# Spectral mixing and a snake MLP on one Trainium2 core: PSUM dealt out by hand, and a burst's halves evicted in one instruction each

## The chip, the cores and the metric

The kernel runs on one core of one Trainium2 chip. The core has TensorE (matrix multiplication, written PE in the profile, its weight loads PEld), VectorE (DVE), ScalarE (ACT), GpSimd (POOL, here mainly an issuer of DMAs) and SyncE (SP, another issuer of DMAs). They run side by side and wait for one another through semaphores. Matmul results land in PSUM, eight banks that hold 512 fp32 columns for each of 128 partitions; VectorE or ScalarE then copies them out ("evicts" them). The metric is device time in microseconds.

## The reference

The input `x` has 8 batches of 3008 positions and 256 channels. It passes a spectral filter along the positions and then a two-layer MLP with a snake activation:

```python
X = np.fft.rfft(x, axis=1)
F = (filt_r + 1j * filt_i)[None, :, :]
y = np.fft.irfft(X * F, n=x.shape[1], axis=1)
h = y.reshape(24064, 256) @ w_in            # 256 -> 2048
s = np.sin(alpha * h)
g = h + s * s / (alpha + 1e-09)
out = g @ w_out                             # 2048 -> 256
```

## The kernel before

**The Fourier part.** 3008 = 47 x 64, so each transform is done in two matmul stages with a pass through DRAM between them. For each batch the stages are: `first` (length 47, tile `pa`), a store to DRAM (`d1`) and a load back in another order (`t2`), `forward` (length 64, tile `pb`, cast to `xf`), the filter product on VectorE (`product`, `cross`; the part that needs swapped halves goes through two SyncE transfers into `xs`), `inverse` (tile `pc`, cast to `g` or `gt`), a store to DRAM (`d2`) and a load (`t4`), and `last` (tile `pd`, cast into `y`). Batch 0 has its own code at the start, batch 1 uses the whole array, and the batches 2 to 7 use the array in quarters.

**Bursts.** For the batches 2 to 7 the stages `first` and `inverse` are written so that four matmuls of a 64x64 quarter of the array can run at once. One call of `first_tiled` issues 8 matmuls, one call of `inverse_tiled` 16. There are 6 x 4 = 24 of the first (called forward bursts below) and 6 x 3 = 18 of the second (inverse bursts), 42 in all. A burst writes four PSUM tiles of 512 columns: two passes q = 0, 1 and in each one tile for each half of the array's rows (h in `first_tiled`, k in `inverse_tiled`). Pass 0 takes both its tiles from the pool `fps`, pass 1 both from `hps`. Each pass is followed in program order by its two evictions. A forward burst has two on ScalarE (h = 0) and two on VectorE (h = 1), an inverse burst three on ScalarE and one on VectorE.

**The MLP part.** The positions are worked through in chunks of 512 (some of 384). For a chunk, `hidden(k, jb)` makes one block of 128 hidden features: two matmuls into a tile `ph` of `hps` (line 601), a cosine on ScalarE into one of four slots of `cos_all` (605), and a VectorE instruction that forms the snake's result `v` from the cosine and from `ph` (606); here sin² is had from a cosine, with the factors folded into the weights. `project(k - 1, u)` multiplies the previous chunk's `v` by the second weight matrix into a tile `po` of `ops` (620), ScalarE copies that to `o` (630), and DMAs store it (665).

**PSUM.** Three pools share the eight banks: `fps` with two tiles, `hps` with four, `ops` with two. Apart from the bursts, `fps` serves `forward` and `last` in the main part, one bank for each call, and `hps` serves `hidden`. A pool hands its banks out in turn; an instruction that writes a bank waits until the bank's last reader is done.

**Order.** Nothing reorders instructions: the program order is written out by hand. The main loop takes steps; a step has two calls of `hidden` (four ph matmuls), a slot, one or more half blocks of `project` (eight po matmuls each), and a second slot. The Fourier stages stand in a list sorted by due time (`put`) and are issued in the slots, normally one TensorE stage for each slot. `clear` moves `forward` and `last` away from the slot of a burst, to a step later, and `aside` moves VectorE's products. Each engine works through its own queue in this order; on SyncE the stores to DRAM, the transfers for `xs` and the loads of `t4` share one queue.

**Who evicts.** `evac` copies a tile out on the engine that its caller names. Where none is named, a counter decides: it goes up by one with every call, whoever makes it, and each third call goes to VectorE. Of the main part's stages only `last` (the casts into `y`) leaves it to the counter.

Of the kernel before, what the change touches and what calls it, by code (L numbers as in the profile page):

```python
# [9 lines left out]
FP16 = mybir.dt.float16  # L10
# [10 lines left out]
N1, N2 = 47, 64  # L21
# [50 lines left out]
def kernel(  # L72
# [44 lines left out]
    dpool = pool("dram", 2, DRAM)  # L117
    fps = pool("fps", 2, PSUM)
    hps = pool("hps", 4, PSUM)
    ops = pool("ops", 2, PSUM)  # L120

# [67 lines left out]
    class Spectral:  # L189
# [13 lines left out]
        def first(self, i):  # L203
            ch, j = divmod(i, 4)
            ps = fps.tile([128, 512], FP32, name=f"pa_{self.b}_{i}", tag="f")
            marks["pe"] = nc.tensor.matmul(out=ps[0:NK, :], lhsT=wf_t, rhs=self.x[ch][:, 2 * j:2 * j + 2, :],
                                           start=True, stop=True)
            r0 = 8 * (ch % 2)
            evac(t1_h[ch // 2][0:NK, r0 + 2 * j:r0 + 2 * j + 2, :], ps[0:NK, :])
            if j == 3:  # L210
                nc.sync.dma_start(out=self.d1_rows[:, 8 * ch:8 * ch + 8, :], 
                                  in_=t1_h[ch // 2][0:NK, r0:r0 + 8, :])

        def first_tiled(self, ch):
            r0 = 8 * (ch % 2)
            for q in range(2):
                own, tag = (hps, "h") if q else (fps, "f")
                ps = [own.tile([128, 512], FP32, name=f"pa_{self.b}_{ch}_{q}_{h}", tag=tag) for h in range(2)]
                for h in range(2):
                    for c in range(2):  # L220
                        n = 4 * c + 2 * q
                        nc.tensor.matmul(out=ps[h][64 * c:64 * c + 64, :], lhsT=wt_t[64 * h:64 * h + N1],  # L222
                                         rhs=self.x[ch][64 * h:64 * h + N1, n:n + 2, :], start=True, stop=True)
                for h in range(2):
                    evac(t1_h[ch // 2][:, r0 + 4 * h + 2 * q:r0 + 4 * h + 2 * q + 2, :], ps[h], h == 0)
            d1 = self.d1.rearrange("a (h n) c -> a h (n c)", h=2)
            for c in range(2):
                n0 = (8 * ch + 4 * c) * C
                nc.sync.dma_start(out=d1[:, :, n0:n0 + 4 * C],
                                  in_=t1_h[ch // 2][64 * c:64 * c + 2 * NS, r0:r0 + 8, :]  # L230
                                  .rearrange("a (h n) c -> a h (n c)", h=2))
# [6 lines left out]
        def forward(self, u):  # L238
            b = self.b
            ps = fps.tile([128, 2, C], FP32, name=f"pb_{b}_{u}", tag="f")  # L240
            for i in range(2):
                s = 2 * u + i
                nc.tensor.matmul(out=ps[:, i, :], lhsT=d_t[:, s, :],  # L243
                                 rhs=self.t2[s // 6][:, s % 6, :], start=True, stop=True)
# [21 lines left out]
        def inverse(self, w):  # L266
            b = self.b
            pr = self.p.pop(w)
            if w % 3 == 0:
                self.g = gpool.tile([128, 6, C], FP16, name=f"g_{b}_{w}", tag="g")  # L270
            ps = fps.tile([128, 2, C], FP32, name=f"pc_{b}_{w}", tag="f")
# [12 lines left out]
        def inverse_tiled(self, w):  # L284
            g = gpool.tile([128, 4, 2, C], FP16, name=f"gt_{self.b}_{w}", tag="g")
            for q in range(2):
                own, tag = (hps, "h") if q else (fps, "f")
                ps = [own.tile([128, 2, C], FP32, name=f"pc_{self.b}_{w}_{q}_{k}", tag=tag) for k in range(2)]
                for i in range(2):
                    for k in range(2):  # L290
                        for c in range(2):
                            u = 4 * w + 2 * c + q
                            nc.tensor.matmul(out=ps[k][64 * c:64 * c + 64, i, :],  # L293
                                             lhsT=eh_t[64 * k:64 * k + 64, 2 * u + i, :],
                                             rhs=self.p[u][0][64 * k:64 * k + 64, i, :], start=True, stop=True)
# [52 lines left out]
    def spread_alpha(i):  # L348

        ps = hps.tile([128, 4, 128], FP32, name=f"al_bc_{i}", tag="h")  # L350
        for a in range(4):
# [40 lines left out]

    def last_0(n0, n, own=fps, tag="f", spread=False):

        for cb in range(2):
            made = []

            def one(i, cb=cb, made=made):

                if i == 0:  # L400
                    ps = own.tile([128, 512], FP32, name=f"pd_0_{n0}_{cb}", tag=tag)
                    made.append(ps[:, 0:n * NR].rearrange("p (a r) -> p a r", r=NR))
                nc.tensor.matmul(out=made[0][:, i, :], lhsT=t4_cols[:, n0 + i, :, cb], rhs=wi0_t,
# [10 lines left out]
    def reciprocals():  # L414

        ps = ops.tile([128, 512], FP32, name="ps_rec", tag="o")
        nc.tensor.transpose(out=ps[:, 0:16], in_=rec, identity=id32)
        nc.vector.tensor_scalar(out=rec_t, in0=ps[:, 0:16], scalar1=-0.5, scalar2=None, op0=ALU.mult)

    def inverse_table(g):  # L420

        gs = slice(8 * g, 8 * g + 8)
        ps = ops.tile([128, 8, 128], FP16, name=f"pse_{g}", tag="o")
        for i in range(8):
# [4 lines left out]

    warmed = []  # L430

    def warm_pe(n):

        warmed.append(n)
        ps = hps.tile([128, 512], FP32, name=f"warm_{len(warmed)}", tag="h")
        for i in range(n):
# [19 lines left out]
    for i in range(16):  # L456
        own, tag = (fps, "f") if i % 3 == 2 else (hps, "h")
        ps = own.tile([128, 512], FP32, name=f"pa_0_{i}", tag=tag)
        nc.tensor.matmul(out=ps, lhsT=wf0_t[0:NR], rhs=x0[i // 4][:, 2 * (i % 4):2 * (i % 4) + 2, :],  # L459
# [27 lines left out]
    def forward_0(i):  # L487
        hc, w = blocks[i]
        ps = hps.tile([128, 4, 128], FP32, name=f"pb_0_{i}", tag="h")
        for j in range(4):  # L490
# [16 lines left out]
    def inverse_0(i):  # L507
        hc, w = blocks[i]
        ps = fps.tile([128, 4, 128], FP32, name=f"pc_0_{i}", tag="f")
        for j in range(4):  # L510
# [73 lines left out]
    last_0(0, 4)  # L584
    last_0(4, 2, hps, "h")
    warm_pe(2)
# [23 lines left out]
    def project(k, u):  # L610
# [6 lines left out]
        if (t % 2 == 0 or final) and half == 0:  # L617
            pso[k] = ops.tile([128, 2, C], FP32, name=f"po_{k}_{t}", tag="o")
        for jb in range(8 * half, 8 * half + 8):
# [79 lines left out]
    for n0, n, at in ((6, 5, 1.5), (11, 4, 11), (15, 4, 13), (19, 4, 15.5), (23, 4, 17), (27, 5, 19)):  # L699
        put(at, last_0, n0, n, fps, "f", True)  # L700
    for b in range(1, B):
# [90 lines left out]
```

## Time and profile before

| What | Value |
|---|---|
| Median of the runs | 778.87 us |
| Lowest of the runs | 777.43 us |
| Profiled execution, its own time | 779.97 us |
| its span, first to last instruction | 778.2 us |
| Granted TensorE clock, mean | 0.997 |
| Matmuls ph (line 601) | 1536, 0.216 us apart in a row |
| Matmuls po (line 620) | 3008, 0.109 us apart in a row |
| Forward burst, 8 matmuls | 0.63 us from its first start to its last end |
| Inverse burst, 16 matmuls | 0.63 us |
| VectorE cast of 128x512 from PSUM | 0.682 us |
| ScalarE cast of 128x512 from PSUM | 0.59 us |
| ScalarE cosine 128x512 / VectorE snake 128x512 | 0.608 / 0.682 us |

Times of a single instruction run from its shown start to its shown end; instructions that follow one another on an engine overlap a little, so a group of two or three is shorter than its sum. A matmul is shown with its way through the array (0.379 us for 512 columns), although the next can start 0.216 us after it. In the chain of work that ended last each piece is counted from the end of the piece before it. The span leaves out 1.8 us of the execution's own time.

### The profile page before, as it was taken

Reading aid. Unit: us, or ns where it says so; the run is one execution under the profiler, and the core shown is the slowest. Engines: PE = TensorE matmul, PEld = TensorE weight load, DVE = VectorE, ACT = ScalarE, POOL = GpSimd, SP = SyncE. Lnnn points to the kernel's source line nnn. Section 1 sums busy time; section 2 is a strip of 40 time slices with the busy share of each in tenths; the row PEclk is TensorE's granted clock in tenths of the full one; section 3 lists DMA queues with packets and bytes.
Section 4 is the critical chain, followed back from the end, with each engine's and each line's share of the span. In section 5 each row is a group of like instructions: output and inputs, shape, how many; then the busy total and the mean of one; then the engine's idle time right before and its main releaser. Section 6 shows DMA issues by size and latency. Waiting matters only on the chain.

```text
span 778.2 us, 17224 instructions
## 1 busy us (share of the span) xinstructions
PE 763.9 (98%) x6039; PEld 517.3 (66%) x6039; DVE 658.2 (85%) x1173; ACT 610.5 (78%) x1203; POOL 371.2 (48%) x649
## 2 busy tenths in 40 slices
PE   8999999999999999999999999999999999999997
PEld 4757766666666666666666666766666666766665
DVE  6986998999988888898889988899888888787773
ACT  5798888898888877888878787788778787777762
POOL 6355554634555655455464647554464655430000
PEclk9999999999999999999999999999999999999999
DMA  9955578854765428644474536764254332411112
GB/s 227 264 110 158 119 179 240 223 137 124 188 164 133 124 58 215 157 108 128 108 202 111 141 93 147 198 150 121 72 145 111 85 72 56 135 46 34 36 41 56
DMA packets 81518, 101.49 MB, mean 130 GB/s; under 512 B 18884, under 2 KB 60864, under 8 KB 81431
## 3 DMA queue, kind: packets, MB, share of 16 engines
q0 software_dynamic: 27440, 47.29, 25.9%
q1 hardware_dynamic: 53434, 52.79, 25.3%
q8 instruction: 47, 0.77, 0.4%
q10 hardware_dynamic: 557, 0.31, 0.2%
q14 instruction: 40, 0.33, 0.1%
HBM read 56.15 MB, written 46.66 MB: 132 GB/s over the span
## 4 chain that ended last, share of the span: by engine, by line
PE 91%; DVE 4%; DMA 2%; ACT 1%; issue 1%; ACTq 0%; POOLq 0%; DVEq 0%
PE po L620 40%; PE ph L601 40%; DVE v L606 3%; PE pd L316 2%; PE pb L243 2%; PE pa L222 2%; PE pc L293 1%; PE pc L513 1%; DMA w<-in_moe_alpha_dram 1%; PE warm L437 1%; DMA d<-t_h 1%; ACT cos_all L605 1%; PE pb L491 1%; DMA t<-d 1%; PE pa L459 1%
## 5 line engine op out<-in xcount | busy, mean ns | idle before, releaser
L606 DVE SCALAR_TENSOR_TENSOR v<-cos_all,ph 128x512 f16<-128x512 f32 (+1 forms) x768 | 482.7, 671 | 96.9 <-ACT cos_all L605 93.1
L605 ACT ACTIVATE cos_all<-ph 128x512 f32<-128x512 f32 (+1 forms) x768 | 413.7, 599 | 100.3 <-PE ph L601 99.8
L665 POOL DMA_DIRECT2D out_dram<-o x530 | 292.5, 558 | 241.8 <-ACT o L630 212.6
L601 PE MATMUL ph<-y,w 128*128 128x512 f16 (+1 forms) x1536 | 389.1, 375 | 1.3 <-DVE v L606 1.1
L620 PE MATMUL po<-w,v 128*128 128x256 f16 x3008 | 389.3, 273 | 0.0
L620 PEld LDWEIGHTS <-v 128*128 128x128 f16 x3008 | 290.1, 98 | 84.2 <-issue 1.1
L601 PEld LDWEIGHTS <-w 128*128 128x128 f16 x1536 | 143.2, 98 | 113.9 <-issue 19.0
L630 ACT COPY o<-po 128x512 f32<-128x512 f32 x94 | 55.9, 595 | 7.6 <-PE po L620 7.3
L246 ACT CAST xf<-pb 128x512 f16<-128x512 f32 x84 | 50.9, 606 | 2.2 <-PE pb L243 1.4
L185 ACT CAST y<-pd 128x376 f16<-128x376 f32 (+1 forms) x86 | 41.9, 490 | 12.2 <-PE pd L316 8.8
L160 POOL DMA_DIRECT2D x<-in_x_dram x48 | 25.6, 539 | 40.5 <-DVE v L606 26.7
L185 ACT CAST t_h<-pa 128x512 f16<-128x512 f32 (+1 forms) x60 | 32.8, 589 | 12.5 <-PE pa L222 11.3
L316 PEld LDWEIGHTS <-t_a 96*128 96x128 f16 x448 | 31.4, 97 | 12.7
L264 DVE TENSOR_TENSOR p<-p,xs 128x512 f16<-128x512 f16 x84 | 35.7, 425 | 2.9
L263 DVE TENSOR_TENSOR xs<-xs,filt_t 128x512 f16<-128x512 f16 x84 | 35.1, 418 | 1.6 <-DMA xs<-xf 1.5
L257 DVE TENSOR_TENSOR p<-xf,filt_t 128x512 f16<-128x512 f16 x84 | 35.0, 418 | 0.0
L185 ACT CAST gt<-pc 128x512 f16<-128x512 f32 x54 | 28.1, 594 | 8.4 <-PE pc L293 8.4
L187 DVE CAST t_h<-pa 128x512 f16<-128x512 f32 (+1 forms) x52 | 33.5, 682 | 0.2
L243 PE MATMUL pb<-t,d_t 128*128 128x256 f16 x168 | 32.1, 273 | 0.8 <-DMA t<-d 0.8
L316 PE MATMUL pd<-wh_t,t_a 96*128 96x94 f16 x384 | 31.8, 204 | 0.0
L235 POOL DMA_DIRECT2D t<-d x28 | 24.4, 873 | 13.2 <-DMA d<-t_h 11.2
L243 PEld LDWEIGHTS <-d_t 128*128 128x128 f16 x168 | 16.3, 98 | 15.3 <-DMA t<-d 1.0
(70 smaller groups left out, 277.9 us busy)
## 6 DMA issues: line engine op xcount, KB each, us to landing
t<-d POOLq DMA_DIRECT2D x28, 384.0 KB, 5.2
xs<-xf SPq DMA_DIRECT2D x168, 64.0 KB
t_a<-d SPq DMA_DIRECT2D x28, 384.0 KB
x<-in_x_dram POOLq DMA_DIRECT2D x50, 188.0 KB, 4.4
d<-t_h SPq DMA_DIRECT2D x48, 192.0 KB
d<-gt SPq DMA_DIRECT2D x36, 256.0 KB
out_dram<-o POOLq DMA_DIRECT2D x91, 64.0 KB, 2.1
out_dram<-o POOLq DMA_DIRECT2D x31, 80.0 KB, 3.8
```

Source lines behind the costliest of these rows:

```text
L185: marks["act"] = nc.scalar.copy(out=dst, in_=src)
L243: nc.tensor.matmul(out=ps[:, i, :], lhsT=d_t[:, s, :], rhs=self.t2[s // 6][:, s % 6, :], start=True, stop=True)
L246: nc.scalar.copy(out=self.xf[u], in_=ps)
L263: nc.vector.tensor_tensor(out=xs, in0=xs, in1=f_t[1][:, 2 * u:2 * u + 2, :], op=ALU.mult)
L264: nc.vector.tensor_tensor(out=p, in0=p, in1=xs, op=ALU.add)
L316: nc.tensor.matmul(out=psv[:, i, :], rhs=wi_t if self.b < TILED else wh_t, start=True, stop=True, lhsT=t4_h[ch // 2][0:NK, n0 % 16 + i, cb ...
L601: nc.tensor.matmul(out=ps[:, 0:n], lhsT=w1[:, cb, jb * 128:jb * 128 + 128], rhs=y_cols[:, cb, c0:c0 + n], start=(cb == 0), stop=(cb == 1))
L605: nc.scalar.activation(out=cs[:, 0:n], in_=ps[:, 0:n], func=AFT.Sin, bias=float(np.pi / 2))
L606: marks["snake"] = nc.vector.scalar_tensor_tensor(out=v[k][:, jb, 0:n], in0=cs[:, 0:n], scalar=-1.0, in1=ps[:, 0:n], op0=ALU.add, op1=ALU. ...
L620: nc.tensor.matmul(out=pso[k][:, t % 2, :], lhsT=v[k][:, jb, 128 * t:128 * t + 128], rhs=w2[:, jb, :], start=(jb == 0), stop=(jb == 15))
L630: copy(out=o[:, i0:t % 2 + 1, :], in_=pso[k][:, i0:t % 2 + 1, :])
L665: queues[i % len(queues)].dma_start(out=bass.AP(tensor=out.tensor, offset=out.offset + t0 * C, ap=[*ap, [1, C]]), in_=o_blk[p0:p0 + rows, :])
```

## The change

The three PSUM pools are replaced by one tile of eight banks. A small class `Ring` deals out the banks of three ranges of it: banks 0 and 1 (`fps`), 2 to 5 (`hps`), 6 and 7 (`ops`). `take(n)` gives n neighbouring banks as one row of n x 512 columns, and rounds its position up to a multiple of n first. All other users of PSUM take single banks in the same order as before.

In the bursts, each half of the array's rows (h or k) now has two neighbouring banks: the first half's are both banks of `fps`, the second half's two of `hps`, and pass q writes columns 512q to 512q + 511. The matmuls come in the same order as before. The evictions now stand behind both passes, and there is one of 1024 columns for each half: in `first_tiled` ScalarE takes the `hps` half and VectorE the `fps` half; in `inverse_tiled` ScalarE takes both, the `hps` half first. As the bursts call `evac` less often, the counter stands elsewhere when `last` asks it.

```diff
-    fps = pool("fps", 2, PSUM)
-    hps = pool("hps", 4, PSUM)
-    ops = pool("ops", 2, PSUM)
+    psum = pool("psum", 1, PSUM).tile([128, 8, 512], FP32, name="psum")
+
+    class Ring:
+
+        def __init__(self, first, n):
+            self.first, self.n, self.at = first, n, 0
+
+        def take(self, n=1):
+            at = -(-self.at // n) * n % self.n
+            self.at = (at + n) % self.n
+            return psum[:, self.first + at:self.first + at + n].rearrange("p b c -> p (b c)")
+
+    fps, hps, ops = Ring(0, 2), Ring(2, 4), Ring(6, 2)
...
         def first_tiled(self, ch):
             r0 = 8 * (ch % 2)
+            ps = [fps.take(2), hps.take(2)]
             for q in range(2):
-                own, tag = (hps, "h") if q else (fps, "f")
-                ps = [own.tile([128, 512], FP32, name=f"pa_{self.b}_{ch}_{q}_{h}", tag=tag) for h in range(2)]
                 for h in range(2):
                     for c in range(2):
                         n = 4 * c + 2 * q
-                        nc.tensor.matmul(out=ps[h][64 * c:64 * c + 64, :], lhsT=wt_t[64 * h:64 * h + N1],
+                        nc.tensor.matmul(out=ps[h][64 * c:64 * c + 64, 512 * q:512 * q + 512],
+                                         lhsT=wt_t[64 * h:64 * h + N1],
                                          rhs=self.x[ch][64 * h:64 * h + N1, n:n + 2, :], start=True, stop=True)
-                for h in range(2):
-                    evac(t1_h[ch // 2][:, r0 + 4 * h + 2 * q:r0 + 4 * h + 2 * q + 2, :], ps[h], h == 0)
+            for h in (1, 0):
+                evac(t1_h[ch // 2][:, r0 + 4 * h:r0 + 4 * h + 4, :], ps[h], h == 1)
...
         def forward(self, u):
             b = self.b
-            ps = fps.tile([128, 2, C], FP32, name=f"pb_{b}_{u}", tag="f")
+            ps = fps.take().rearrange("p (i c) -> p i c", c=C)
...
         def inverse_tiled(self, w):
             g = gpool.tile([128, 4, 2, C], FP16, name=f"gt_{self.b}_{w}", tag="g")
+            ps = [r.take(2).rearrange("p (j c) -> p j c", c=C) for r in (fps, hps)]
             for q in range(2):
-                own, tag = (hps, "h") if q else (fps, "f")
-                ps = [own.tile([128, 2, C], FP32, name=f"pc_{self.b}_{w}_{q}_{k}", tag=tag) for k in range(2)]
                 for i in range(2):
                     for k in range(2):
                         for c in range(2):
                             u = 4 * w + 2 * c + q
-                            nc.tensor.matmul(out=ps[k][64 * c:64 * c + 64, i, :],
+                            nc.tensor.matmul(out=ps[k][64 * c:64 * c + 64, 2 * q + i, :],
                                              lhsT=eh_t[64 * k:64 * k + 64, 2 * u + i, :],
                                              rhs=self.p[u][0][64 * k:64 * k + 64, i, :], start=True, stop=True)
-                for k in range(2):
-                    evac(g[:, 2 * q:2 * q + 2, k, :], ps[k], (q, k) != (1, 1))
+            for k in (1, 0):
+                evac(g[:, :, k, :], ps[k], True)
...
-            ps = fps.tile([128, 4, 128], FP32, name=f"pd_{self.b}_{u}", tag="f")
-            psv = ps.rearrange("p a b -> p (a b)")[:, 0:4 * NR].rearrange("p (a r) -> p a r", r=NR)
+            psv = fps.take()[:, 0:4 * NR].rearrange("p (a r) -> p a r", r=NR)
...
-        ps = hps.tile([128, 512], FP32, name=f"ph_{k}_{jb}", tag="h")
+        ps = hps.take()
```

More of the change, by code (lines that the diff above doesn't have):

```diff
@@ L204, in first @@
             ch, j = divmod(i, 4)
-            ps = fps.tile([128, 512], FP32, name=f"pa_{self.b}_{i}", tag="f")
+            ps = fps.take()
             marks["pe"] = nc.tensor.matmul(out=ps[0:NK, :], lhsT=wf_t, rhs=self.x[ch][:, 2 * j:2 * j + 2, :],
@@ L270, in inverse @@
                 self.g = gpool.tile([128, 6, C], FP16, name=f"g_{b}_{w}", tag="g")
-            ps = fps.tile([128, 2, C], FP32, name=f"pc_{b}_{w}", tag="f")
+            ps = fps.take().rearrange("p (i c) -> p i c", c=C)
             for i in range(2):
@@ L348, in spread_alpha @@
     def spread_alpha(i):
-        ps = hps.tile([128, 4, 128], FP32, name=f"al_bc_{i}", tag="h")
+        ps = hps.take().rearrange("p (a b) -> p a b", b=128)
         for a in range(4):
@@ L391, in one_between, with last_0 @@
             between.pop(0)()
-    def last_0(n0, n, own=fps, tag="f", spread=False):
+    def last_0(n0, n, own=fps, spread=False):
         for cb in range(2):
@@ L400, in one @@
                 if i == 0:
-                    ps = own.tile([128, 512], FP32, name=f"pd_0_{n0}_{cb}", tag=tag)
-                    made.append(ps[:, 0:n * NR].rearrange("p (a r) -> p a r", r=NR))
+                    made.append(own.take()[:, 0:n * NR].rearrange("p (a r) -> p a r", r=NR))
                 nc.tensor.matmul(out=made[0][:, i, :], lhsT=t4_cols[:, n0 + i, :, cb], rhs=wi0_t,
@@ L414, in reciprocals @@
     def reciprocals():
-        ps = ops.tile([128, 512], FP32, name="ps_rec", tag="o")
+        ps = ops.take()
         nc.tensor.transpose(out=ps[:, 0:16], in_=rec, identity=id32)
@@ L422, in inverse_table @@
         gs = slice(8 * g, 8 * g + 8)
-        ps = ops.tile([128, 8, 128], FP16, name=f"pse_{g}", tag="o")
+        ps = ops.take().bitcast(FP16).rearrange("p (a b) -> p a b", b=128)
         for i in range(8):
@@ L428, in inverse_table @@
         nc.scalar.mul(e1_0[:, gs, :], ps, -0.125)
-    warmed = []
     def warm_pe(n):
-        warmed.append(n)
-        ps = hps.tile([128, 512], FP32, name=f"warm_{len(warmed)}", tag="h")
+        ps = hps.take()
         for i in range(n):
@@ L456 @@
     for i in range(16):
-        own, tag = (fps, "f") if i % 3 == 2 else (hps, "h")
-        ps = own.tile([128, 512], FP32, name=f"pa_0_{i}", tag=tag)
+        ps = (fps if i % 3 == 2 else hps).take()
         nc.tensor.matmul(out=ps, lhsT=wf0_t[0:NR], rhs=x0[i // 4][:, 2 * (i % 4):2 * (i % 4) + 2, :],
@@ L488, in forward_0 @@
         hc, w = blocks[i]
-        ps = hps.tile([128, 4, 128], FP32, name=f"pb_0_{i}", tag="h")
+        ps = hps.take().rearrange("p (s c) -> p s c", c=128)
         for j in range(4):
@@ L508, in inverse_0 @@
         hc, w = blocks[i]
-        ps = fps.tile([128, 4, 128], FP32, name=f"pc_0_{i}", tag="f")
+        ps = fps.take().rearrange("p (s c) -> p s c", c=128)
         for j in range(4):
@@ L584 @@
     last_0(0, 4)
-    last_0(4, 2, hps, "h")
+    last_0(4, 2, hps)
     warm_pe(2)
@@ L598, in hidden @@
             v[k] = vpool.tile([128, 16, 512], FP16, name=f"v_{k}", tag="v")
-        ps = hps.tile([128, 512], FP32, name=f"ph_{k}_{jb}", tag="h")
+        ps = hps.take()
         for cb in range(2):
@@ L617, in project @@
         if (t % 2 == 0 or final) and half == 0:
-            pso[k] = ops.tile([128, 2, C], FP32, name=f"po_{k}_{t}", tag="o")
+            pso[k] = ops.take().rearrange("p (t c) -> p t c", c=C)
         for jb in range(8 * half, 8 * half + 8):
@@ L699 @@
     for n0, n, at in ((6, 5, 1.5), (11, 4, 11), (15, 4, 13), (19, 4, 15.5), (23, 4, 17), (27, 5, 19)):
-        put(at, last_0, n0, n, fps, "f", True)
+        put(at, last_0, n0, n, fps, True)
     for b in range(1, B):
```

## The prediction

> **What bounds the kernel now.** I read the engine shares, then the chain of work that ended last, then the waits, then the timeline around single bursts.
>
> The first part of the page and its chain:
>
> ```profile
> PE 763.9 (98%) x6039; PEld 517.3 (66%) x6039; DVE 658.2 (85%) x1173; ACT 610.5 (78%) x1203; POOL 371.2 (48%) x649
> ...
> PE 91%; DVE 4%; DMA 2%; ACT 1%; issue 1%; ACTq 0%; POOLq 0%; DVEq 0%
> ```
>
> Busy PE alone proves little, since matmuls are pipelined; the chain says it: 91% of the span is TensorE working off its own queue. In the list of waits, TensorE's hidden-layer matmuls (ph) waited for VectorE only 4 times, 1.1 us in all. So TensorE has no idle time for a change to remove, and every new TensorE wait lengthens the run by itself.
>
> The chain of waits, in order of time, around one inverse burst (start us, us, what):
>
> ```profile
> 446.72 0.56 PE pc L293 x16
> 447.28 0.97 PE ph L601 x4
> 448.25 0.87 PE po L620 x8
> 449.12 0.17 PE pd L316 x4
> 449.29 0.86 PE ph L601 x4
> ```
>
> No gap between the pieces. After a burst always come four ph matmuls (bank ring of four), and sooner or later the next user of the two-bank ring f: a forward (pb) or last (pd) stage.
>
> The timeline around a forward burst and an inverse burst (start us, us, engine, line, what, [idle before]):
>
> ```profile
> 408.71 0.63 PE L222 MATMUL pa<-x,wt_t 47*64 47x512 f16 x8
> 409.16 1.07 ACT L185 CAST t_h<-pa 128x512 f16<-128x512 f32 x2 [0.56 <-PE pa L222]
> 409.35 1.28 DVE L187 CAST t_h<-pa 128x512 f16<-128x512 f32 x2
> 410.14 0.38 PE L243 MATMUL pb<-t,d_t 128*128 128x256 f16 x2
> ...
> 414.98 0.63 PE L293 MATMUL pc<-p,e_t 64*64 64x256 f16 x16
> 415.42 1.56 ACT L185 CAST gt<-pc 128x512 f16<-128x512 f32 x3 [0.56 <-PE pc L293]
> 415.68 0.69 DVE L187 CAST gt<-pc 128x512 f16<-128x512 f32 x1
> 416.41 0.33 PE L316 MATMUL pd<-wh_t,t_a 96*128 96x94 f16 x4
> 416.86 1.12 ACT L605 ACTIVATE cos_all<-ph 128x512 f32<-128x512 f32 x2
> ```
>
> Two things are to be seen. ScalarE starts evicting 0.45 us after the burst's start, while its second half still runs, because the first half fills ring f alone. And the next user of ring f follows the burst's start by only 1.43 us in both cases: 410.14 and 416.41.
>
> **The evictions, part by part.** After the change each eviction reads both halves, so none can start before the burst ends (0.63 us after its start S). An engine starts about 0.04 us after its last matmul's shown end: at 413.14 a ph group starts, its second matmul 0.216 later and 0.379 long, so it ends at 413.74, and the cosine starts at 413.78. A waiting matmul starts 0.05 us after its release: a snake of VectorE ended at 136.60 and the matmul behind it started at 136.66.
>
> The 1024-column casts aren't in the trace. VectorE: 512 columns 0.682, 376 columns 0.542, 188 columns 0.343, so 1.05 ns a column and 0.682 + 512 x 1.05 = 1.22 us. Bounds: 0.83 (its 94x1024 cast, which reads SBUF) and 2 x 0.682 = 1.36. I take 1.22, since those rows read PSUM. ScalarE: 512 columns 0.59, 376 columns 0.49: 0.59 + 512 x 0.8 = 1.02, near its own 128x1024 row (1.04, f16 source). Bounds 0.99 (the low slope, 0.765 ns) and 2 x 0.59 = 1.19. Two in a row overlap by about 0.1 (three casts took 1.56).
>
> - Forward burst, 24 times. Ring f is now evicted whole by VectorE: start S + 0.67 (its snakes are done at S + 0.71, and a cast follows its predecessor 0.07 early), end S + 1.89, TensorE may go on at S + 1.94. It arrives at S + 1.43: **0.51 us new wait**. Today the bank needed first is ScalarE's first cast, free about S + 1.04.
> - Inverse burst, 18 times. ScalarE evicts ring h first, then f: S + 0.67 to 1.69, then 1.59 to 2.61; release S + 2.66. If the f user comes right behind the four ph: S + 1.44, **1.23 us**. If eight po stand between: S + 2.31, **0.36 us**. If a second ph group does too: S + 3.17, nothing.
>
> I went through all 42 bursts with these terms, each with its own VectorE start and arrival. Forward: 20 have the f user directly behind the ph group; 13 cost 0.50, seven cost 0.53 to 0.72, because VectorE was late or TensorE early there: 11.2 us. In four another user comes at S + 2.46 or later, after its release: 0. Inverse: three at 1.24, two at 0.83 (f user at S + 1.96, late start): 5.4 us; six with po between at 0.37: 2.2 us; seven at nothing. **Sum 18.8 us**, in 31 waits.
>
> What is queued behind. On ScalarE the cosines stand behind the wide cast: S + 1.41 becomes 1.60 (forward), S + 1.89 becomes 2.53 (inverse). They feed the snakes, which free the ph banks. In the inverse case the snakes would end at S + 3.85 and 4.45; TensorE wants these banks again at S + 4.35 and 4.57 at the earliest (two ph groups and two po groups on). That is 0.07 us of room in the tightest order, so I cost it at nothing and keep it as a rival. On TensorE, behind the waiting pb or pd stands everything: it issues in order, so the wait is paid in full. SP's stores of gt leave 0.6 us later and of t_h no later; the exchange transfers (xs) queued behind them depend on casts that come later anyway.
>
> **What costs nothing.** The built program has the same order of TensorE instructions as before, so the hand-dealt block moves no matmul; waits name the same readers. Rounding ring f up to bank 0 makes a burst's first matmul wait for the youngest f user: in the trace that one's cast had ended 0.4 us or more before S at all bursts but the first (0.17). Ring h's first bank is now needed at S and not a quarter microsecond later; it was free 0.3 us or more before S at all 42. VectorE loses 18 inverse casts (12.4 us) and saves about 24 x 0.14 (3.5 us) by merging; the eviction counter that picks the engine shifts, and 12 casts of y go from ScalarE to VectorE (+6.5). VectorE nets -9.4 us, ScalarE about -5. Both lie beside TensorE: worth nothing on the path.
>
> The row against the skill: VectorE is 85% busy and ScalarE 78%, TensorE owns the chain. The Trainium skill, "Perfetto Trace Analysis", section "Optimizing Scalar/DVE Operations", says that grouping into larger operations can help when that engine is saturated, and that breaking up lets work complete sooner when it isn't saturated but holds up others. By these shares the second half applies here. The same page's "Matmuls" asks for groups to rotate through banks so that eviction overlaps the next group; the cast starting at S + 0.45 is such an overlap, and by that rule giving it up costs. By the grouping half alone the sum would be rival 3's; by the other two rules the 18.8 us stand, and the trace agrees so far as its chain is TensorE's.
>
> **The rivals.**
> 1. Late cosines reach the ph banks. For: room of 0.07 us. Against: most bursts have 0.24 or more, and a TensorE wait of 1.23 swallows the 0.64 us delay. Price: 7 x 0.64 + 6 x 0.27 = 6.1 us more, some 804 us. Chance 0.13.
> 2. Wide casts are cheap. With 0.83 on VectorE the forward waits fall by 0.39 each to 3.4 us; with 0.99 on ScalarE the inverse ones to 6.9: 10.3 us, some 789 us. For: a 1024-column cast at that rate exists. Against: it reads SBUF, the PSUM rows all have 1.05 ns a column. Chance 0.12.
> 3. Not slower: VectorE, not TensorE, sets the pace. Then TensorE would reach the f user after its release, nothing would wait, and VectorE's 9.4 us would come off: about 770 us. It decides from the point where TensorE comes 0.51 us later behind a forward burst and 1.23 behind an inverse one than it does now. For: VectorE busy 8 or 9 tenths of most slices. Against: 1.1 us of waits for it. Chance 0.05. The skill's grouping rule, above, would be this case.
> 4. The evictions are not really wide, or TensorE's f user is elsewhere: the built program shows 24 + 60 casts of 1024 columns and the f users in the same places. Time as before; chance 0.02.
>
> **The numbers.** The profiled execution took 779.97 us (span 778.2 and 1.8 around it); with 18.8 it is 798.8. The median of the runs shown is 1.1 lower, 778.87, so I give **798 us**, chance 0.68. The range must take in the wide casts' bounds: below, 789 (rival 2); above, either 1.36 on VectorE (20 x 0.14, +2.9) or 1.19 on ScalarE (11 x 0.34, +3.7) together with rival 1 makes about 807; all three at once, 810, I leave out. So 789 to 807; outside lie rivals 3, 4 and tails, under 2 in 10. A measurement tells a change from none at about 2%: 794.5 us is that border. Slower: most of the forecast's own case (0.62) and rival 1: 0.75. Within 2%: rivals 2 and 4 and the forecast's lower tail: 0.20. Faster: 0.05.
>
> **What the changed profile would show.** A new wait of TensorE's f users, pb and pd, for VectorE's t_h cast (some 20 of 0.5 to 0.7 us) and for ScalarE's gt cast (5 of about 1.2 or 0.8, 6 of 0.4); TensorE's share down from 98% to about 96; t_h casts of 128x1024 near 1.22 on VectorE, gt near 1.02 on ScalarE; 36 gt casts, none on VectorE; ph waits for snakes still about 1 us. If ph waits grow by several us, rival 1 is right; if casts are short, rival 2; if the f users wait for nothing, I have misjudged where TensorE arrives.

## The result, and the profile after

The changed kernel takes 801.63 us against 778.15 us for the kernel before in the same comparison: a ratio of **1.0296, 95% interval 1.0274 to 1.0319**. It is slower. Both times are medians of four executions, of which one each is far off (999.83 us at a granted clock of 0.753, and 2804.09 us); the ratio is of the others, 800.27 to 802.18 us after the change and 777.26 to 778.87 us before.

The first part of its page (busy time and share of each engine) and its chain of work that ended last:

```profile
PE 768.6 (96%) x6039; PEld 517.1 (65%) x6039; DVE 651.8 (82%) x1143; ACT 613.2 (77%) x1149; POOL 371.5 (47%) x649
...
PE 72%; DVE 14%; DMA 5%; ACT 5%; issue 2%; POOL 1%; SPq 0%; ACTq 0%; DVEq 0%; POOLq 0%
```

The matmuls are the same 6039, VectorE (DVE) has 30 instructions fewer and ScalarE (ACT) 54 fewer, and their busy time has gone from 658.2 to 651.8 us and from 610.5 to 613.2. TensorE's part of the chain fell from 91% to 72%, and the rest passes now mostly through VectorE, DMA and ScalarE. VectorE got less work and came onto the path. How much time was lost can't be read from these shares: 19 points are some 130 us, and the run got 23 longer. The waits tell that.

The list of waits (engine, line, releaser: us in total, times, longest) has these new lines of TensorE:

```profile
PE psum L324 <- ACT gt L195: 5.7, 10, 1.1
...
PE psum L253 <- DVE t_h L197: 5.6, 12, 0.6
...
PE psum L324 <- DVE t_h L197: 3.4, 8, 0.6
```

L253 is `forward` (pb), L324 is `last` (pd): both users of ring f, waiting for the wide casts of the bursts. These are 30 waits, 14.7 us; a pb that waits 0.2 us for a `gt` cast makes 31. This view counts only the time in which TensorE shows nothing running. A matmul is shown for 0.38 us but lets the next one start after 0.22, so each such wait is some 0.16 us longer if it is counted from start to start.

The timeline of the kernel after around one forward and one inverse burst (start us, us, engine, line, what, [idle before]):

```profile
420.68 0.63 PE L231 MATMUL psum<-x,wt_t 47*64 47x512 f16 x8
...
421.24 1.04 PE L604 MATMUL psum<-y,w 128*128 128x512 f16 x4
421.34 1.23 DVE L197 CAST t_h<-psum 128x1024 f16<-128x1024 f32 x1
421.38 1.01 ACT L195 CAST t_h<-psum 128x1024 f16<-128x1024 f32 x1 [0.82 <-PE psum L231]
...
422.62 0.38 PE L253 MATMUL psum<-t,d_t 128*128 128x256 f16 x2 [0.35 <-DVE t_h L197]
...
427.44 0.63 PE L302 MATMUL psum<-p,e_t 64*64 64x256 f16 x16
...
428.01 1.04 PE L604 MATMUL psum<-y,w 128*128 128x512 f16 x4
428.12 1.93 ACT L195 CAST gt<-psum 128x1024 f16<-128x1024 f32 x2 [0.80 <-PE psum L302]
...
430.10 0.33 PE L324 MATMUL psum<-wh_t,t_a 96*128 96x94 f16 x4 [1.06 <-ACT gt L195]
```

Forward: burst at 420.68, ring f's cast ends at 422.57, the waiting pb starts at 422.62, that is S + 1.94; before, this user came at S + 1.43. Inverse: burst at 427.44, two wide casts in a row to 430.05, the pd at 430.10, S + 2.66.

The groups by form give the casts' own durations (busy us, mean ns of one | idle before):

```profile
L195 ACT CAST gt<-psum 128x1024 f16<-128x1024 f32 x36 | 34.7, 1015 | 13.2 <-PE psum L302 13.2
...
L197 DVE CAST t_h<-psum 128x1024 f16<-128x1024 f32 x24 | 29.3, 1220 | 0.8 <-PE psum L231 0.8
...
L195 ACT CAST t_h<-psum 128x1024 f16<-128x1024 f32 x24 | 24.3, 1012 | 17.4 <-PE psum L231 17.4
```

**Where the time went.** The order of TensorE's instructions is the same in both kernels, so the two traces can be laid side by side: for each matmul I took how much later it starts after the one ahead of it than in the kernel before. I count from the first ph matmul of the main loop to the last one, since the profiled execution of before reached the first at 38.39 us and all others of this study at 36.0 to 36.5. From there the kernel before takes 725.8 us, the kernel after 748.2: 22.4 more.

| Delay of TensorE, start to start | us |
|---|---|
| ring f's user, first behind a forward burst, 20 waits | 12.3 |
| ring f's user, first behind an inverse burst, 11 waits | 7.65 |
| ahead of the first burst (batch 1) | 0.85 |
| in the bursts themselves (the first waits 0.86 for a snake) | 0.7 |
| other users of ring f (one pb waits 0.7 for a cast of `y`) | 0.6 |
| ph, for VectorE's snakes | 0.5 |
| rest | -0.2 |

The profiled time itself grew by 20.3 us only (779.97 to 800.27), because of that late start of the one profiled execution of before.

### The profile page after: what moved, and what is told of

It is laid out like the page before. It is cut to its first block, busy times and chain, and to the rows that moved or that the text cites. A ratio compares the mean times of both kernels' runs of the same rounds, so it can differ in the third digit from the quotient of the medians.

```text
span 798.5 us, 17220 instructions
## 1 busy us (share of the span) xinstructions
PE 768.6 (96%) x6039; PEld 517.1 (65%) x6039; DVE 651.8 (82%) x1143; ACT 613.2 (77%) x1149; POOL 371.5 (47%) x649
## 4 chain that ended last, share of the span: by engine, by line
PE 72%; DVE 14%; DMA 5%; ACT 5%; issue 2%; POOL 1%; SPq 0%; ACTq 0%; DVEq 0%; POOLq 0%
PE psum L623 34%; PE psum L604 31%; DVE v L609 9%; DVE t_h L197 3%; PE psum L324 2%; ACT gt L195 2%; PE psum L253 2%; ACT cos_all L608 2%; DMA d_t<-d_tbl 1%; PE psum L302 1%; DMA w_out<-in_moe_w_out_dram 1%; DMA filt_t<-in_filt_r_dram 1%; DMA out_dram<-o 1%; DMA w_in<-in_moe_w_in_dram 1%; DVE p L267 1%
## 5 line engine op out<-in xcount | busy, mean ns | idle before, releaser
L609 DVE SCALAR_TENSOR_TENSOR v<-cos_all,psum 128x512 f16<-128x512 f32 (+1 forms) x768 | 482.2, 671 | 125.4 <-ACT cos_all L608 123.2
L608 ACT ACTIVATE cos_all<-psum 128x512 f32<-128x512 f32 (+1 forms) x768 | 411.0, 594 | 106.6 <-PE psum L604 103.9
L604 PE MATMUL psum<-y,w 128*128 128x512 f16 (+1 forms) x1536 | 389.8, 375 | 1.0 <-DVE v L609 0.7
L623 PE MATMUL psum<-w,v 128*128 128x256 f16 x3008 | 389.3, 273 | 0.0
L633 ACT COPY o<-psum 128x512 f32<-128x512 f32 x94 | 54.9, 584 | 11.1 <-PE psum L623 8.5
L195 ACT CAST t_h<-psum 128x1024 f16<-128x1024 f32 (+2 forms) x48 | 38.9, 817 | 20.0 <-PE psum L231 17.4
L256 ACT CAST xf<-psum 128x512 f16<-128x512 f32 x84 | 50.5, 601 | 2.5 <-PE psum L253 1.9
L324 PEld LDWEIGHTS <-t_a 96*128 96x128 f16 x448 | 31.3, 97 | 24.6 <-issue 13.6
L195 ACT CAST gt<-psum 128x1024 f16<-128x1024 f32 x36 | 34.7, 1015 | 13.2 <-PE psum L302 13.2
L195 ACT CAST y<-psum 128x376 f16<-128x376 f32 (+1 forms) x74 | 35.5, 479 | 10.2 <-PE psum L324 6.7
L324 PE MATMUL psum<-wh_t,t_a 96*128 96x94 f16 x384 | 31.8, 204 | 7.0 <-ACT gt L195 5.7
L253 PE MATMUL psum<-t,d_t 128*128 128x256 f16 x168 | 32.0, 272 | 6.3 <-DVE t_h L197 5.6
L253 PEld LDWEIGHTS <-d_t 128*128 128x128 f16 x168 | 16.3, 98 | 22.9 <-issue 10.1
```

Source lines behind the costliest of these rows:

```text
L195: marks["act"] = nc.scalar.copy(out=dst, in_=src)
L253: nc.tensor.matmul(out=ps[:, i, :], lhsT=d_t[:, s, :], rhs=self.t2[s // 6][:, s % 6, :], start=True, stop=True)
L324: nc.tensor.matmul(out=psv[:, i, :], rhs=wi_t if self.b < TILED else wh_t, start=True, stop=True, lhsT=t4_h[ch // 2][0:NK, n0 % 16 + i, cb ...
L604: nc.tensor.matmul(out=ps[:, 0:n], lhsT=w1[:, cb, jb * 128:jb * 128 + 128], rhs=y_cols[:, cb, c0:c0 + n], start=(cb == 0), stop=(cb == 1))
L608: nc.scalar.activation(out=cs[:, 0:n], in_=ps[:, 0:n], func=AFT.Sin, bias=float(np.pi / 2))
L609: marks["snake"] = nc.vector.scalar_tensor_tensor(out=v[k][:, jb, 0:n], in0=cs[:, 0:n], scalar=-1.0, in1=ps[:, 0:n], op0=ALU.add, op1=ALU. ...
```

## The experiments

All diffs are against the kernel after, with parts left out at the dots. The table gives the median, the kernel before in the same comparison, and the ratio.

| Kernel | us | before | ratio, 95% |
|---|---|---|---|
| e1, the block and the rings alone | 779.83 | 777.35 | 1.0031 (1.0019 to 1.0042) |
| e2, wide evictions in forward bursts only | 791.67 | 777.35 | 1.0185 (1.0169 to 1.0200) |
| e3, in inverse bursts only | 787.45 | 777.35 | 1.0133 (1.0118 to 1.0148) |
| e4, inverse: ring f evicted first | 797.90 | 777.34 | 1.0250 (1.0222 to 1.0279) |
| e5, late but narrow evictions | 784.64 | 777.35 | 1.0094 (1.0079 to 1.0109) |
| e6, wide but early: one per pass | 784.95 | 777.34 | 1.0084 (1.0051 to 1.0116) |
| e7, ring f's users later | 789.12 | 777.34 | 1.0142 (1.0114 to 1.0170) |
| e8, e1 with the pools' order of banks | 777.80 | 778.51 | 0.9992 (0.9977 to 1.0007) |
| e9, ring f's users moved both ways | 786.36 | 778.51 | 1.0097 (1.0075 to 1.0120) |
| e10, as e9, the products where they were | 784.82 | 778.84 | 1.0078 (1.0059 to 1.0097) |

### e1: the block alone

The block and the rings stay; the bursts go back to single banks with a 512-column cast for each, behind each pass.

```diff
-            ps = [fps.take(2), hps.take(2)]
             for q in range(2):
+                own = hps if q else fps
+                ps = [own.take() for h in range(2)]
...
-            for h in (1, 0):
-                evac(t1_h[ch // 2][:, r0 + 4 * h:r0 + 4 * h + 4, :], ps[h], h == 1)
+                for h in range(2):
+                    evac(t1_h[ch // 2][:, r0 + 4 * h + 2 * q:r0 + 4 * h + 2 * q + 2, :], ps[h], h == 0)
...
-            for k in (1, 0):
-                evac(g[:, :, k, :], ps[k], True)
+                for k in range(2):
+                    evac(g[:, 2 * q:2 * q + 2, k, :], ps[k], (q, k) != (1, 1))
```

> PSUM as one block with rings dealt out by hand, but the bursts and their 512-column evictions as before. Theory (the wide evictions hold ring f too long): the block costs nothing, 778 us within 2, no wait of pb or pd. Rival (dealing out one block makes the waits coarser or rounds a bank away): most of the 23 us stay, 790 us or more.

Measured: 779.83 us, 2.5 above before, and the interval of the ratio excludes 1. Start to start it is 2.2 us: 0.85 ahead of the bursts, 1.03 in bursts, 0.47 at users of ring f, ph -0.15. So my "nothing" for the block is not quite right. Its list of waits has lines that the kernel before does not have:

```profile
PE psum L216 <- DVE t_h L197: 1.4, 1, 1.4
...
PE psum L232 <- DMA x<-in_x_dram: 0.6, 2, 0.4
```

The second one is the 1.03 us in bursts: a single forward burst, at 144 us, that waited for its load of `x`. It is not a wait for a bank, and no other trace here waits so at that burst; whether the order of banks has a part in it is not shown. The timeline of e1 at the place of the first line, batch 1's third `first` matmul (start us, us, engine, line, what, [idle before]):

```profile
47.74 0.68 DVE L197 CAST t_h<-psum 96x512 f16<-96x512 f32 x1
...
48.48 0.38 PE L216 MATMUL psum<-x,wf_t 94*96 94x512 f16 x1 [1.40 <-DVE t_h L197]
```

The same matmul in the kernel before, where it waits for ScalarE's cast instead:

```profile
49.27 0.58 ACT L185 CAST t_h<-pa 96x512 f16<-96x512 f32 x1
...
49.90 0.38 PE L206 MATMUL pa<-x,wf_t 94*96 94x512 f16 x1 [0.43 <-ACT t_h L185]
```

It writes another bank than before, whose reader is another engine. That is what e8 follows up.

### e2 and e3: one kind of burst each

e2 has e1's inverse bursts and the wide evictions in the forward ones; e3 has it the other way round.

```diff
e2, in inverse_tiled:
-            for k in (1, 0):
-                evac(g[:, :, k, :], ps[k], True)
+                for k in range(2):
+                    evac(g[:, 2 * q:2 * q + 2, k, :], ps[k], (q, k) != (1, 1))
e3, in first_tiled:
-            for h in (1, 0):
-                evac(t1_h[ch // 2][:, r0 + 4 * h:r0 + 4 * h + 4, :], ps[h], h == 1)
+                for h in range(2):
+                    evac(t1_h[ch // 2][:, r0 + 4 * h + 2 * q:r0 + 4 * h + 2 * q + 2, :], ps[h], h == 0)
```

> Block and wide evictions in the forward bursts alone; inverse bursts as before. Theory: the 20 waits behind forward bursts stay, 12.3 us by the changed kernel's trace, and the first burst's 0.6: about 791 us. Rival (late cosines behind two wide casts of ScalarE are the cost): only inverse bursts have them, so about 780 us.

> Block and wide evictions in the inverse bursts alone; forward bursts as before. Theory: the 11 waits behind inverse bursts, 7.6 us by the changed kernel's trace, and at most 1 us of ph waits: about 786 us. Rival (late cosines): nearly the whole 23 us, about 800 us.

Measured: e2 791.67, e3 787.45. Above e1 that is 11.8 and 7.6 us, where the terms of the prediction were 11.2 and 7.6. Start to start, ring f's users wait 11.65 us behind the forward bursts of e2 and 7.11 behind the inverse bursts of e3. That the inverse part comes out at 7.6 is in part luck: the trace of e3 has also 1.6 us more of ph waits than e1's, and lacks the 1.03 us of the late load. The parts nearly add up: 2.5 + 11.8 + 7.6 = 21.9, and the kernel after is 23.5 above before; the 1.6 between was not assigned.

### e5: late, but narrow

The layout, the order and the engines of the kernel after, but each half is evicted in two instructions of 512 columns. The casts start as late as the wide ones; the bank that is needed first comes free after half the time.

```diff
             for h in (1, 0):
-                evac(t1_h[ch // 2][:, r0 + 4 * h:r0 + 4 * h + 4, :], ps[h], h == 1)
+                for q in range(2):
+                    evac(t1_h[ch // 2][:, r0 + 4 * h + 2 * q:r0 + 4 * h + 2 * q + 2, :],
+                         ps[h][:, 512 * q:512 * q + 512], h == 1)
...
             for k in (1, 0):
-                evac(g[:, :, k, :], ps[k], True)
+                for q in range(2):
+                    evac(g[:, 2 * q:2 * q + 2, k, :], ps[k][:, 2 * q:2 * q + 2, :], True)
```

> The changed kernel's bank layout, order and engines, each half evicted behind both passes, but by two 512-column casts. Theory (one instruction holds both banks of ring f to its end): bank 0 is free after the first narrow cast, behind forward bursts at S + 1.40 against an arrival at S + 1.43; behind inverse bursts at S + 2.27, so five waits of 0.4 to 0.8 stay; some 4 us in all, about 782 us. Rival (the late start behind both passes alone is the cost): about 800 us.

Measured: 784.64 us, 7.3 above before in place of 23.5; 16 us are back. The timeline of e5 at a forward burst:

```profile
411.52 0.63 PE L231 MATMUL psum<-x,wt_t 47*64 47x512 f16 x8
412.00 1.07 ACT L195 CAST t_h<-psum 128x512 f16<-128x512 f32 x2 [0.60 <-PE psum L231]
412.07 1.04 PE L607 MATMUL psum<-y,w 128*128 128x512 f16 x4
412.15 1.28 DVE L197 CAST t_h<-psum 128x512 f16<-128x512 f32 x2
412.95 0.38 PE L255 MATMUL psum<-t,d_t 128*128 128x256 f16 x2
```

VectorE works on until 413.43, nearly as long as with one wide cast, but the pb is there at S + 1.43 and waits for nothing: its bank was free after the first of the two. Start to start, ring f's users wait 1.44 us in all behind forward bursts and 2.13 behind inverse ones. It missed its 782 by 2.6 us. The expected waits of some 4 us are there (3.6); besides them the trace has 1.4 us ahead of the bursts and at other users of ring f, as e1 has, 0.9 in the first burst and 0.9 at ph. The counter of `evac` stands here as in the kernel before, so e5 undoes the shift of the `y` casts too; at most the 1.1 us by which the forward waits of the kernel after exceed the forecast can hang on that.

### e6: wide, but early

Here the pair of banks belongs to a pass instead of a half: pass 0 fills both banks of ring f, one wide cast on ScalarE takes them while pass 1 fills ring h.

```diff
-            ps = [fps.take(2), hps.take(2)]
+            t1 = t1_h[ch // 2][:, r0:r0 + 8, :].rearrange("p (h q n) c -> p q h (n c)", h=2, q=2)
             for q in range(2):
+                ps = (hps if q else fps).take(2).rearrange("p (h m) -> p h m", h=2)
...
-            for h in (1, 0):
-                evac(t1_h[ch // 2][:, r0 + 4 * h:r0 + 4 * h + 4, :], ps[h], h == 1)
+                evac(t1[:, q], ps, q == 0)
...
-            for k in (1, 0):
-                evac(g[:, :, k, :], ps[k], True)
+                evac(g[:, 2 * q:2 * q + 2, :, :].rearrange("p i k c -> p k i c"), ps, True)
```

> Wide casts of 1024 columns, but one for each pass: pass 0 fills both banks of ring f (one for each half of the rows), ScalarE evicts them at once, pass 1 fills ring h (VectorE in the forward, ScalarE in the inverse burst). Theory (it is the f ring's release against the next f user's arrival): cast from S + 0.45, release S + 1.52 against an arrival at S + 1.43, so 25 waits of about 0.1 and a few of 0.3: 3 to 4 us, about 781 us. Rival (width itself is the cost, whatever it starts): about 795 us or more.

Measured: 784.95 us, 4 above the 781 expected. The timeline of e6 at a forward burst:

```profile
412.39 0.63 PE L232 MATMUL psum<-x,wt_t 47*64 47x512 f16 x8
412.85 1.01 ACT L195 CAST t_h<-psum 128x1024 f16<-128x1024 f32 x1 [0.57 <-PE psum L232]
412.95 1.04 PE L602 MATMUL psum<-y,w 128*128 128x512 f16 x4
413.07 1.22 DVE L197 CAST t_h<-psum 128x1024 f16<-128x1024 f32 x1
413.92 0.38 PE L252 MATMUL psum<-t,d_t 128*128 128x256 f16 x2
```

The casts are as wide as in the kernel after, but ring f's starts at S + 0.46 instead of S + 0.66 and is on the faster engine; the pb starts at S + 1.53. Ring f's users wait 2.16 us behind forward and 0.27 behind inverse bursts. That is half of what keeps it above e1; the other half is at ph matmuls, which are delayed by 2.23 us. Together, e5 and e6 say: neither the late start alone nor the width alone costs the 20 us. A late start together with a full width does, since the first user has 1.43 us of room and the sum takes 1.94 or 2.66. In the forward bursts e6 changes the engine as well, and that counts: behind its snakes VectorE starts its first cast only at S + 0.64 even in the kernel before (409.35 - 408.71), so an early wide cast on VectorE would release ring f at about S + 1.91 (0.64 + 1.22 + 0.05; an estimate, not run), hardly sooner than in the kernel after. It is ScalarE that can start early there.

### e4: the inverse bursts evict ring f first

```diff
-            for k in (1, 0):
+            for k in (0, 1):
                 evac(g[:, :, k, :], ps[k], True)
```

> The changed kernel with the inverse burst's two wide casts the other way round: ring f first, then ring h. Theory: ring f comes free at S + 1.74 in place of S + 2.66, so five waits fall by 0.92 to 0.3 and six of 0.35 vanish, 6.7 us less than the changed kernel, about 794 us; ring h is wanted at about S + 2.6, no new wait above 0.2 us. Rival (late cosines): the cosines start as late as before, so no gain, about 801 us.

Measured: 797.90 us, a miss by 4. Half of the mechanism is as expected: ring f's users behind inverse bursts wait 0.88 us in place of 7.65. But now ring h comes free last, and its users are the ph matmuls. The list of waits of e4:

```profile
PE psum L604 <- DVE v L609: 0.9, 3, 0.6
...
PE psum L604 <- ACT gt L195: 0.9, 5, 0.2
```

The second line is in no other list of waits of the study (start to start e6 has 0.8 us of it too). Start to start, ph matmuls are delayed 26 times, 4.77 us in all, 2.8 of it in 11 waits of about a quarter of a microsecond for the `gt` cast, the rest for snakes. So of the 6.8 us that ring f won, 4.3 were lost at the ph matmuls (4.77 in place of 0.5). The order with h first is therefore not free either: whichever ring goes second pays.

### e7: ring f's users later

`clear` moved `forward` and `last` out of a burst's own slot; here also out of the next one, a step and a half behind the burst. One product is left out: with the late `forward`, one unit of batch 2 (unit 7) has its swapped-halves product added only after the inverse burst has read its sum. The same holds for e9.

```diff
-        return next((s + 1 for s in bursts if s - 0.75 < at <= s + 0.25), at)
+        return next((s + 1.5 for s in bursts if s - 0.75 < at <= s + 1.1), at)
```

> The changed kernel's evictions untouched; forward and last stages that were due within one step behind a burst are put half a step or a step later, so that two ph and one or two po groups stand between a burst and the next user of ring f (arrival at S + 3.17, release at S + 1.94 or 2.66). Theory: all waits for ring f vanish, 778 to 781 us. Rival (engine load, late cosines or the block are the cost): about 800 us.

Measured: 789.12 us, 8 above the upper end expected. All 31 waits for wide casts are gone. The list of waits of e7 shows what took their place:

```profile
PE psum L253 <- DVE y L197: 2.0, 2, 1.4
...
PE psum L604 <- DVE v L609: 1.5, 5, 0.6
```

Users of ring f that were put off crowd behind one another and wait for VectorE's casts of `y` (9 delays, 4.2 us start to start, the longest 1.5 and 0.7), and ph matmuls wait for snakes (6.6 us in all, 1.9 in the kernel before). With the 0.85 us ahead of the bursts that is 9.8 of the 12.7 us by which it exceeds before between first and last ph; the other 2.9 were not assigned.

### e8: the block with the pools' own order of banks

In e1, 2736 of 6039 matmuls write another bank than in the kernel before. By the built program a pool does not give its banks plainly in turn, as I described it (hps starts with 2, 5, 4, 3, 2, 4, 3, 5); it seems to give the one that it got back first. e8 is e1 with the block's banks dealt from lists, read off the kernel before; with them every matmul writes the same bank as there.

```diff
-        def __init__(self, first, n):
-            self.first, self.n, self.at = first, n, 0
+        def __init__(self, first, places):
+            self.first, self.places = first, iter(places)
 
-        def take(self, n=1):
-            at = -(-self.at // n) * n % self.n
-            self.at = (at + n) % self.n
-            return psum[:, self.first + at:self.first + at + n].rearrange("p b c -> p (b c)")
+        def take(self):
+            return psum[:, self.first + int(next(self.places))]
...
```

> The block alone, as in e1, but each bank is dealt out in the order in which the pools of the kernel before gave it (read off its program and written as a list); the warm-up call with no matmul takes no bank. Theory (the 2 us of e1 come from the rings' own order, by which a stage asks for the bank that was written last where the pools gave the one that was freed first): back to the time of before, 777.4 us within 0.7. Rival (one block with its own waits costs 2 us whatever the order): about 779.7 us.

Measured in 12 runs: 777.80 us against 778.51, ratio 0.9992, interval 0.9977 to 1.0007. The 2.2 us are gone; from first to last ph it takes 724.9 us, before 725.8. Between the first and the last ph none of e1's added waits is left, the late load of `x` among them. So one tile of eight banks costs nothing by itself, and the rest of e1's loss is the order in which the rings deal.

### e9 and e10: the same evictions, the users moved both ways

`forward` of the batches 2 to 7 moves later, `last` moves earlier, so that they don't crowd as in e7. e10 also leaves `cross` where it was.

```diff
+    def later(at):
+        return next((s + 1.5 for s in bursts if s - 0.75 < at <= s + 1.1), at)
+
+    def sooner(at):
+        return next((s - 1.5 for s in bursts if s - 0.75 < at <= s + 1.1), at)
...
-            fwd = clear(fwd)
+            old = clear(fwd)
+            fwd = later(fwd) if b > 1 else old
...
-                put(aside(fwd + (4 if b == 1 else 4.5)), s.cross, u)
+                put(aside(old + (4 if b == 1 else 4.5)), s.cross, u)
...
-            put(clear(z + (u - (5 if b == 1 else 6.5) if u < 4 else 2 * u - 9 if b == 1 else 2.6 * u - 11)),
+            put((sooner if b > 1 else clear)(z + (u - (5 if b == 1 else 6.5) if u < 4 else 2 * u - 9 if b == 1 else 2.6 * u - 11)),
```

(e9 has the first, second and last of these edits, with `cross` at `fwd` still.)

> The changed kernel's evictions untouched, output complete: forward stages due within a step behind a burst go 1.5 steps behind it, last stages due there go 1.5 steps ahead of it (for batches 2 to 7). Theory: the 31 waits for ring f behind bursts (20.0 us) vanish and the block's own 2 us stay, 780 to 783 us. Rival (engine load or late cosines): the time moves to ph waits, 790 us or more.

> As e9, with the products of each forward unit kept at the place that they have in the changed kernel, so that the output is whole. Theory: the waits for ring f behind bursts stay gone from batch 2's last stages on (batch 1's are not moved: four forward and one inverse burst wait, 2.9 us), the block's 2 us and about 3 us of ph waits stay: 785 us, 16 us under the changed kernel. Rival (the gain of e9 came from the part that was read too early): back to about 800 us.

Measured: e9 786.36, a miss by 3; e10 784.82, as expected. The first part of e10's page, and its list of waits:

```profile
PE 764.8 (98%) x6039; PEld 517.1 (66%) x6039; DVE 642.5 (82%) x1128; ACT 615.5 (79%) x1164; POOL 371.8 (47%) x649
```

```profile
PE psum L324 <- DVE t_h L197: 1.9, 4, 0.6
PE psum L604 <- DVE v L609: 1.5, 5, 0.6
...
PE psum L253 <- DVE y L197: 0.7, 1, 0.7
...
PE psum L324 <- ACT gt L195: 0.2, 1, 0.2
```

TensorE is back at 98%. The five waits that are left belong to batch 1's `last`, which was not moved. Between the start of the 14th burst and that of the 42nd, where no such wait is left, the kernel before takes 426.6 us, the kernel after 442.1, e10 427.8. So the same wide evictions at the same times, from the same block, cost 1.2 us there in place of 15.5 once nobody asks for their bank early. (e1 takes 426.6 us there: the order of banks costs its time ahead of that stretch.) None of these versions beats the kernel before; e8 equals it.

## Why the prediction came out as it did

The forecast of 798 us was 3.6 short, and 801.63 lies in the range of 789 to 807. Point by point:

- **The two new waits: right.** Release at S + 1.94 and S + 2.66 was forecast, and at the two bursts shown 422.62 - 420.68 and 430.10 - 427.44 are that to the hundredth. 31 waits were counted, and 31 are there.
- **Inverse term: right**, 7.6 forecast, 7.65 in the trace: three waits of 1.22, two of 0.94 (0.83 forecast) and six of 0.35. In e3 alone ring f's waits are 7.11.
- **Forward term: under-sized by a tenth**, 11.2 forecast, 12.3 in the trace (11.65 in e2). At five bursts VectorE's snakes ahead of the wide cast ended 0.3 to 0.4 us later than in the kernel before, and the wait is 0.70 there in place of 0.50. The prediction had worked with VectorE's old start times. What put VectorE behind (the 12 more casts of `y` that the counter gives it, or the later cosines) was not separated.
- **The price of a wide cast: right.** 1.220 us on VectorE (I took 1.22) and 1.015 on ScalarE (1.02). By these rows rival 2 fell: PSUM is read at the rate of the 512-column rows, not at that of the 94x1024 row from SBUF.
- **Rival 3, VectorE sets the pace: fell.** VectorE lost 6.4 us of busy time and the run got 23 us longer. The second half of the rule in the Trainium skill, "Perfetto Trace Analysis", section "Optimizing Scalar/DVE Operations" (where VectorE and ScalarE aren't saturated but hold up another engine, breaking up may let work complete sooner), is what e5 did to the kernel after, and the trace agrees: with VectorE 82% busy, 16 us came back from 84 evictions cut in two.
- **What merging saves: over-sized, without effect on the time.** I counted 0.14 us for a pair on VectorE, the difference of 2 x 0.682 and 1.220. But two casts in a row overlap: the profiles show 1.28 us for two and 1.23 for one wide one, 1.07 and 1.01 on ScalarE. A merge saves the engine 0.05 to 0.06 us, and holds the first bank 0.4 to 0.5 us longer. VectorE's busy time fell by 6.4 us where 9.4 was forecast, and ScalarE's rose by 2.7 where it was to fall by about 5.
- **Rival 1, late cosines: mostly fell.** It was priced at 6.1 us; ph is delayed by 0.5 in the kernel after. That the waits of 1.23 us on TensorE swallow it was the argument against it, and no run tests that alone; in e4, where these waits are mostly gone and the cosines as late, ph waits 2.0 us for snakes. Its bank did count in e4, mostly by another way: not late cosines, but the late release of ring h itself (2.8 us).
- **"What costs nothing": wrong in two points.** "The hand-dealt block moves no matmul; waits name the same readers" was taken from the order of TensorE's instructions. The order is the same, the banks are not, and so neither are the readers. e1 measured it at 1.0031 (2.5 us), e8 took it back to 0.9992; in e1's trace 1.3 us lie at users that wait for another reader than before. And ring h's first bank was to be free 0.3 us or more before S at all 42 bursts; in the kernel after the first burst waits 0.86 us for a snake that still reads it. Of the whole prediction, this term at nothing is the step that failed.

The sum: 18.8 us of waits forecast, 19.95 there, and 2.45 more ahead of and in the bursts, at other users of ring f and at ph, which the prediction had at nothing. That makes 22.4, and the difference to 18.8 is the 3.6 us by which the forecast was short. The medians differ by 23.5; the 1.1 us between was not assigned.

## What to carry to other kernels

What an eviction costs a kernel whose TensorE never idles is not its engine time, but when the next user's bank comes free: one instruction over two banks holds both until its end, so before merging, look up who writes the first of these banks next and how long after the burst. If the evictions must be wide, start them on the pair of banks that fills first and on the engine that is free then (e6), or move the next user out of their reach (e10), and look at the bank released second as well (e4). Both still took 6 to 8 us more than the kernel before, so of what was tried here narrow evictions behind each pass remain best. When pools are replaced by banks dealt by hand, compare which bank each instruction gets, not only the order of instructions.

## What the runs showed that was not expected

- The order in which banks are dealt is worth 0.3% with the same work in the same order: 1.0031 (1.0019 to 1.0042) dealt in turn, 0.9992 (0.9977 to 1.0007) in the pools' order.
- Moving users out of the way can cost nearly what it saves: e7 removed 20 us of waits and is still 11.8 us above before, 8.9 of it in new waits for casts of `y` and for snakes; moved in two directions (e10), the kernel is 6.0 us above before.
- One 1024-column cast from PSUM is hardly cheaper for its engine than two of 512 in a row: 1.23 against 1.28 us on VectorE, 1.01 against 1.07 on ScalarE.
